# Attention with a selective bias, then a hard-swish MLP: the queries of the first eight pairs in another order

## The chip, the cores and the metric

The kernel runs on one core of a Trainium2 chip. The metric is the device time of one execution in microseconds, as the median of several executions. The engines are named as in the profile: PE multiplies matrices (PEld is its weight load), DVE is the vector engine, ACT the scalar engine, POOL is GpSimd, and SP issues DMAs. All of them run in the order of their own instruction lists and wait for each other by semaphores.

## The reference

Eight batches of eight heads attend causally over 576 tokens of 64 features. The scores carry a bias, minus the difference of running sums of the positive part of `s`, so a key far back in a stretch of large `s` counts less. The result, 4608 rows of 512, goes through two dense layers with a hard-swish between them.

```python
scores = scale * np.matmul(q, k.transpose(0, 1, 3, 2))        # scale = 1/8
cum = np.cumsum(np.maximum(s, 0.0), axis=-1)
bias = -(cum[:, :, :, None] - cum[:, :, None, :])
scores = np.where(causal, -1000000000.0, scores + np.minimum(bias, 0.0))
attn = softmax(scores)                                        # over the keys
x = (attn @ v) as rows of 512                                 # batch and token by head and feature
h = x @ w_in                                                  # 512 -> 2048
out = (h * np.clip(h + 3.0, 0.0, 6.0) / 6.0) @ w_out          # 2048 -> 512
```

## The kernel before

**Pairs.** The 64 heads are taken as 32 pairs `p`; four pairs make a batch of 576 rows. The loop `for p in range(NP)` (L773) writes out the order of work by hand; nothing reorders it. For each pair the queries and keys are loaded (`load_qk`, L109), turned so that features lie on partitions (`transpose_in` on PE, L229, then `transpose_out`, L249, out of PSUM into the tile `qk`), multiplied into scores (`scores`, L310, three groups a head of up to 512 columns, and `corner`, L369, for the last 64 tokens), exponentiated on ACT (L355), multiplied with the values (`av`, L401) and divided by their sums (`norm`, L429). The result `x` of a pair is turned back (`transpose_x`, L444) into `xT`. The loop fetches pair p+1 with `get(0)` (queries) and `get(1)` (keys) while pair p is scored, and does the second head's `av` and `norm` of pair p-1 there as well.

**Three kinds of pairs.** Pairs 0 to 10 (`NPE` is 11) are loaded six tokens to a row of a 96-row tile `tok`, in float16, by POOL's queue. Six PE transposes of 96x128 give a PSUM tile `pt` with two parities of tokens, one on partitions 0 to 63 and one on 64 to 127, and the copies out put them in order: each writes every second token in groups of three. Later pairs use a transposing DMA (`crossbar_qk`) and `spread` (L219). Pairs 0 to 7 (`NPROD` is 8) get their causal mask by product: PE first multiplies a constant tile `shut`, which holds -65504 where a key comes after its query, into the scores (L318, L374). Later pairs have `shut_out` on POOL put zeros in instead. Pairs from 8 on also use a tile of steps (`set_stair`).

**The bias.** Four rows of `qk` (partitions 64 to 67) hold the running sums of queries and keys, so the bias comes out of the same product as the scores. `rows_of` is where the sums are kept for all heads, with one slot for queries and one for keys; `load_aug` (L148) sends a head's rows from there by DMA. For pair 0 alone that would come too late, so its bias comes from a product with all rows (`by_rows`, L301), in which `picked` holds the sums of one head and zeros elsewhere: `pick_first` on ACT (L723) for head 0, `pick(1)` on DVE (L711) for head 1.

**The start.** The running sum over `s` is taken in two halves (`HALVES`, L54), the steps `cum1` to `cum6` (L671 to L702) alternating between ACT and DVE. POOL then copies the query sums into their slot (L747). Pair 0 is copied out head by head (`head_out`, L270), with ACT on three of the eight copies and DVE on five, DVE then does the pick (L756), and POOL goes on with `load_aug(1)`, the value cast of pair 0 (`cast_v`, L193), and further loads.

**Where the work overlaps.** In pairs 0 to 3 there is attention alone. From pair 4 on, `group()` puts one group of the MLP between the pieces of attention, either four matmuls into `ph` (L478, then ACT L493 and DVE L494 for the hard swish) or four into `po` (L505), in the order of the hand-written list `plan`. When a tile of 128 output rows is complete, DVE scales it into `ob` (L521) and SP's queue stores it (L524). SP's queue also issues the loads of values, the transposing DMAs and a few rows of sums; POOL's queue issues the loads that change type (queries and keys, weights) and most of the sums. `pool_mid` (L803) is POOL's share in the middle of a pair: the value cast, and for pairs 5 to 7 the tile of steps.

Of the kernel before, what the change touches and what calls it, by code (L numbers as in the profile page):

```python
# [18 lines left out]
def kernel(  # L19
# [32 lines left out]
    NROW = 1  # L52
    NWARM = (11, 2, 6)
    HALVES = (slice(0, 288), slice(288, SEQ))  # L54

# [35 lines left out]
    ident = keep("ident", [128, 128], F16)  # L91
    shut = keep("shut", [128, 640], F16)
    ident2 = keep("ident2", [128, 128], F16)
    stair_sb = keep("stair_sb", [128, 2, 128], F16)
    bias3 = keep("bias3", [128, 1], F32)
    rows_of = keep("rows_of", [128, 2, 640], F16, 2)
    sel = keep("sel", [128, 4], F32)
# [11 lines left out]
    def load_qk(p, i):  # L109
        b, h0 = p // PPB, 2 * (p % PPB)  # L110
        src = (q, k)[i][b, h0 : h0 + 2]
        if not flat(p):
            if not i:
                tok = work.tile([128, 24 * D], F16, tag="tok", bufs=4, name="tok")
                toks[p] = tok[0:96].rearrange("p (i h e d) -> p i h e d", i=2, h=2, e=6)
            nc.gpsimd.dma_start(
                out=toks[p][:, i].rearrange("p h e d -> p h (e d)"),
                in_=src.rearrange("h (p e) d -> p h (e d)", e=6),
            )
        else:  # L120
            if p < NSW:
                if not i:
                    tok = work.tile([128, 24 * D], F16, tag="tok", bufs=4, name="tok")
                    toks[p] = tok[:, 0 : 18 * D]
                to, eng = toks[p], nc.gpsimd
            else:
                to, eng = raws[p % NRAW], nc.sync
            eng.dma_start(
                out=to.rearrange("p (i t d) -> p i t d", i=2, t=9)[:, i],
                in_=src.rearrange("h s d -> (h s) d").rearrange(  # L130
                    "(t p) d -> p t d", p=128
                ),
            )
# [14 lines left out]
    def load_aug(p, eng):  # L148
        for hh in range(2):
            g = 2 * p + hh  # L150
            eng.dma_start(  # L151
                out=qks[p % NQK][64:68, hh, :, 64 * hh : 64 * hh + SEQ],
                in_=rows_of[g // 32].rearrange("(r g) i t -> g r i t", g=32)[
                    g % 32, :, :, 0:SEQ
                ],
            )
# [72 lines left out]
    def transpose_in(p, i):  # L229
        tok = toks[p]  # L230
        pt = t_bank(i == 1 and p != NPROD, "pt")
        if flat(p):
            for c in range(5):
                c0 = 512 * i + 128 * c
                nc.tensor.transpose(
                    pt[:, 128 * c : 128 * (c + 1)], tok[:, c0 : c0 + 128], ident
                )
            return pt
        for hh in range(2):
            for c in range(3):  # L240
# [6 lines left out]
        return pt  # L247

    def transpose_out(  # L249
        p, i, pt, copies=(nc.vector.tensor_copy, nc.vector.tensor_copy), pars=(0, 1)  # L250
    ):
        qk = qks[p % NQK]
        if flat(p):
            order(qk, i, pt.rearrange("p (t c) -> p t c", c=128), i, copies)
            return
        copies = (nc.scalar.copy if i else copies[0], copies[1])
        for par in pars:
            to = qk[0:64, 0, i, par : par + SEQ]
            copies[par](  # L259
# [9 lines left out]

    def head_out(p, i, hh, pt, copies):  # L270
        to = qks[p % NQK][0:64, hh, i, 64 * hh : 64 * hh + SEQ]
        for par in range(2):
            copies[par](
# [27 lines left out]
    def by_rows(p, hh, out, keys, queries, stop=False):  # L301
        mm(
            out,
            lhsT=rows_of[0][:, 1, keys],
            rhs=picked[:, 2 * p + hh, queries],
# [4 lines left out]
    def scores(p, hh, g):  # L310
# [4 lines left out]
        if g == 0:  # L315
            rows = slice(0, 68 if by_product else 128)
            if by_product:
                mm(S, lhsT=ident2, rhs=shut[:, 0:512], start=True, stop=False)  # L318
            for j in range(4):
# [12 lines left out]
        else:  # L332
# [10 lines left out]
            if p < NROW:  # L343
                for j in ((0, 3) if g == 1 else (1, 2)):
# [3 lines left out]
                        S[:, c : c + w],  # L348
                        lhsT=rows_of[0][:, 1, 128 * j : 128 * (j + 1)],
                        rhs=picked[:, 2 * p + hh, 128 * (j + 1) : SEQ],  # L350
# [18 lines left out]
    def corner(p):  # L369
# [3 lines left out]
        if by_product:  # L373
            mm(  # L374
                S.rearrange("p h c -> p (h c)"),
                lhsT=ident2,
                rhs=shut[:, 512:640],
                start=True,
                stop=False,
            )  # L380
# [117 lines left out]
    def m2(n, i):  # L498
# [13 lines left out]
        if fq == 3:  # L512
# [10 lines left out]
            )  # L523
            nc.sync.dma_start(out=out[r : r + 128, 0:w], in_=ob[:, 0:w])  # L524

# [82 lines left out]
    fill(nc.gpsimd, shut, 0.0)  # L608
    for c in (slice(0, 512), slice(512, 640)):
        w = 128 if c.start == 0 else 64  # L610
        part = shut[:, c].rearrange("p (t c) -> p t c", c=w)
        nc.gpsimd.affine_select(
            out=part,
            in_=part,
            pattern=[[0, (c.stop - c.start) // w], [1, w]],
            compare_op=ALU.is_ge,
            fill=-65504.0,
            base=0,
            channel_multiplier=-1,
        )  # L620

# [24 lines left out]
    fill(nc.gpsimd, rows_of[0][:, 0, :], 1.0)  # L646
    fill(nc.gpsimd, rows_of[0][:, 1, SEQ:640], 0.0)
    fill(nc.gpsimd, qks[0][64:68, 1, :, :], 0.0)
# [37 lines left out]
    def cum3(n, copy, cols):  # L686
        copy(out=rows_of[n][:, 1, cols], in_=C["c"][:, cols])

    def cum4(n, eng, cols):
        eng.tensor_tensor(  # L690
            out=C["r"][64:128, cols],
            in0=C["c"][64:128, cols],
            in1=rows_of[n][64:128, 1, cols],
            op=ALU.subtract,
        )

    def cum5(n, copy, cols):
        copy(out=rows_of[n][64:128, 1, cols], in_=C["r"][64:128, cols])

    def cum6(n, eng, cols):  # L700
        lo = rows_of[n][96:128, 1, cols]
        eng.tensor_tensor(out=lo, in0=C["r"][96:128, cols], in1=lo, op=ALU.subtract)  # L702
# [7 lines left out]

    def pick(g):  # L711
        nc.vector.tensor_scalar(
            out=picked[:, g, :],
# [10 lines left out]
    def pick_first(cols):  # L724
        nc.scalar.activation(
            out=picked[0:32, 0, cols],
            in_=C["c"][0:32, cols],
            func=AF.Identity,
# [7 lines left out]
    cum3(0, A, HALVES[1])  # L736
    fill(nc.gpsimd, rows_of[0][0:32, 1, 0:SEQ], -1.0)
    for i in range(2):
# [7 lines left out]
    pick_first(HALVES[1])  # L746
    nc.gpsimd.tensor_copy(out=rows_of[0][0:32, 0, 0:SEQ], in_=C["c"][0:32])  # L747
    pts = [transpose_in(0, 0)]
# [3 lines left out]
    head_out(0, 1, 0, pts[1], (V.tensor_copy, V.tensor_copy))  # L752
    head_out(0, 0, 1, pts[0], (A, V.tensor_copy))
    head_out(0, 1, 1, pts[1], (V.tensor_copy, V.tensor_copy))
    warm(NWARM[2])
    for g in range(1, 2 * NROW):  # L756
        pick(g)
    load_aug(1, nc.gpsimd)
# [14 lines left out]
    for p in range(NP):  # L773
# [58 lines left out]
        if PPB <= p < NPROD:  # L832
            pool_mid()
            if p == 4:
                load_aug(7, nc.gpsimd)
            elif p in (6, 7):
                load_aug(p + 2, nc.gpsimd)
# [5 lines left out]
        if p == 10:  # L843
            load_s(1, (nc.sync,) * 4)
            fill(nc.gpsimd, rows_of[1][:, 0, :], 1.0)

# [95 lines left out]
        elif p == 12:  # L942
            nc.scalar.copy(out=rows_of[1][0:32, 0, 0:SEQ], in_=C["c"][0:32])
            cum3(1, nc.scalar.copy, whole)
            fill(nc.gpsimd, rows_of[1][0:32, 1, 0:SEQ], -1.0)
        av(p, 0, 1)
# [43 lines left out]
```

The softmax here doesn't subtract the row's maximum and nothing guards it: scores larger than these inputs give would overflow.

## Time and profile before

| what | us |
|---|---|
| median of 3 runs (lowest, highest) | 356.13 (356.01, 356.2) |
| the profiled execution | 356.22 |
| its span, first to last instruction | 354.5 |
| PE busy in the span | 345.6 |
| DVE, ACT, POOL busy in the span | 231.5, 225.4, 169.6 |
| first score product of pair 0 (L318) | 8.95 |
| first score product of pairs 1, 2, 3, 4 (L318) | 14.26, 18.42, 22.68, 26.94 |

All times inside a profile count from the first instruction of the span. In lines of the timeline the columns are start, length, engine, line of the code, operation, what is written and read, shapes, count, and in brackets the idle time before with what ended it. In lines of waits they are who waited, for whom, total, times and longest. In group lines the busy time and the mean of one follow the bar, and then the idle time before them. An engine's name with a q is its sequencer or queue. The granted PE clock is 1.00 throughout. A busy PE isn't a PE at its peak, since matmuls overlap: a matmul of 512 columns shows 379 ns, but four in a row take 0.86 us.

### The profile page before, as it was taken

To read this page: it belongs to the slowest core of one execution; us is meant where nothing else is said; L and a number is where in the kernel's file an instruction comes from. 1 tells how busy PE (TensorE), PEld (TensorE's weight loads), DVE (VectorE), ACT (ScalarE), POOL (GpSimd) and SP (SyncE) were. 2 spreads that over 40 slices of the span, in tenths; PEclk is the share of its full clock that TensorE was granted. 3 is DMA by queue.
4 is the path that set the end of the run, shared out by engine and by line. 5 is a ranking of instruction groups with operands and counts; after the bars stand their busy time and mean duration, and the time that the engine had idled before them with its cause. 6 is when DMAs were issued, how large, how long until landed. Compare 5 with 4: busy or idle time off the path is not lost.

```text
span 354.5 us, 7771 instructions
## 1 busy us (share of the span) xinstructions
PE 345.6 (97%) x2926; PEld 191.5 (54%) x2926; DVE 231.5 (65%) x472; ACT 225.4 (64%) x397; POOL 169.6 (48%) x295
## 2 busy tenths in 40 slices
PE   7889999999999999999999999999999999999995
PEld 3676666655555555555555555555555444444442
DVE  7898897677878677666666665757654553544531
ACT  6897896787787666667766666666664344433310
POOL 8987799666779556555555555555310000000000
PEclk9999999999999999999999999999999999999999
DMA  9999999999999999998788969997120100101111
GB/s 164 156 219 209 186 184 175 104 187 183 146 126 140 190 219 187 160 214 178 174 176 189 179 162 187 175 176 164 39 75 12 59 31 31 59 2 59 59 58 63
DMA packets 144438, 48.35 MB, mean 136 GB/s; under 512 B 130696, under 2 KB 139432, under 8 KB 144400
## 3 DMA queue, kind: packets, MB, share of 16 engines
q1 hardware_dynamic: 117088, 37.52, 53.4%
q0 software_dynamic: 27072, 10.05, 25.4%
q8 instruction: 23, 0.38, 0.5%
q10 hardware_dynamic: 240, 0.28, 0.2%
q14 instruction: 15, 0.12, 0.1%
HBM read 37.36 MB, written 9.44 MB: 132 GB/s over the span
## 4 chain that ended last, share of the span: by engine, by line
PE 90%; DVE 4%; ACT 3%; issue 1%; DMA 1%; ACTq 0%
PE po L505 34%; PE ph L478 34%; PE O L412 8%; PE S L336 7%; PE S L321 4%; DVE qk L259 1%; PE pt L242 1%; ACT P L355 1%; PE ptx L449 1%; DMA s_all<-in_s_dram 1%; DVE x L435 1%; PE S L318 1%; ACT tr L493 1%; DVE qk L219 1%; PE Sc L385 0%
## 5 line engine op out<-in xcount | busy, mean ns | idle before, releaser
L494 DVE SCALAR_TENSOR_TENSOR gT<-tr,ph 128x512 f16<-128x512 f32 x144 | 98.9, 687 | 97.4 <-ACT tr L493 96.3
L478 PE MATMUL ph<-xT,w_in_sb 128*128 128x512 f16 x576 | 148.1, 379 | 0.0
L505 PE MATMUL po<-w_out_sb,gT 128*128 128x512 f16 x576 | 145.8, 379 | 0.0
L493 ACT ACTIVATE tr<-ph,bias 128x512 f32<-128x512 f32 x144 | 99.1, 688 | 73.0 <-PE ph L478 70.6
L355 ACT ACTIVATE P<-S 128x512 f16<-128x512 f32 x192 | 111.4, 596 | 37.4 <-PE S L321 22.2
L478 PEld LDWEIGHTS <-w_in_sb 128*128 128x128 f16 x576 | 51.6, 97 | 44.2
L505 PEld LDWEIGHTS <-gT 128*128 128x128 f16 x576 | 50.2, 97 | 46.4 <-issue 0.2
L359 POOL TENSOR_SCALAR_AFFINE_SELECT P<-P 128x512 f16<-128x512 f16 x48 | 31.2, 650 | 45.2 <-ACT P L355 45.1
L336 PE MATMUL S<-qk 68*128 68x448 f16 (+3 forms) x256 | 49.0, 272 | 0.3 <-ACT P L355 0.2
L412 PE MATMUL O<-va,P 128*128 128x65 f16 x896 | 47.9, 193 | 0.3 <-ACT P L355 0.3
L412 PEld LDWEIGHTS <-P 128*128 128x128 f16 x896 | 39.3, 97 | 14.0 <-ACT P L355 0.5
L219 DVE COPY qk<-jt 64x768 f16<-64x768 f16 x84 | 36.6, 437 | 1.2
L336 PEld LDWEIGHTS <-qk 68*128 68x128 f16 x256 | 23.7, 98 | 24.2 <-issue 0.7
L151 POOL DMA_DIRECT2D qk<-rows_of x58 | 34.1, 591 | 2.8 <-PE S L336 1.6
L435 DVE TENSOR_TENSOR x<-O,rl 128x320 f16<-128x320 f32 x64 | 31.5, 492 | 2.2
L521 DVE TENSOR_SCALAR ob<-po 128x512 f32<-128x512 f32 (+1 forms) x36 | 24.4, 676 | 8.3 <-PE po L505 7.6
L259 DVE COPY qk<-pt 64x576 f16<-64x576 f16 x30 | 24.0, 805 | 6.4 <-ACT qk L259 5.3
L359 POOL TENSOR_SCALAR_AFFINE_SELECT PC<-PC 128x128 f16<-128x128 f16 x24 | 7.1, 294 | 41.0 <-ACT PC L393 40.9
L321 PEld LDWEIGHTS <-qk 128*128 128x128 f16 (+1 forms) x256 | 18.9, 98 | 12.7 <-DVE qk L259 0.8
L321 PE MATMUL S<-qk 128*128 128x128 f16 (+1 forms) x256 | 24.8, 219 | 0.0
L195 POOL CAST va<-vraw 128x512 f16<-128x512 f32 x32 | 21.2, 664 | 3.4 <-DMA vraw<-in_v_dram 3.3
L191 POOL CAST tok<-raw 128x576 f16<-128x576 f32 x28 | 18.1, 681 | 0.0
(71 smaller groups left out, 197.4 us busy)
## 6 DMA issues: line engine op xcount, KB each, us to landing
out_dram<-ob SPq DMA_DIRECT2D x35, 256.0 KB, 2.2
vraw<-in_v_dram SPq DMA_DIRECT2D x64, 128.0 KB, 3.8
raw<-in_q_dram SPq DMA_DIRECT2D x14, 288.0 KB, 3.7
raw<-in_k_dram SPq DMA_DIRECT2D x14, 288.0 KB
tok<-in_q_dram POOLq DMA_DIRECT2D x18, 144.0 KB, 4.9
tok<-in_k_dram POOLq DMA_DIRECT2D x18, 144.0 KB, 6.0
w_in_sb<-in_moe_w_in_dram POOLq DMA_DIRECT2D x4, 512.0 KB, 8.7
w_out_sb<-in_moe_w_out_dram POOLq DMA_DIRECT2D x8, 256.0 KB, 7.4
```

Source lines behind the costliest of these rows:

```text
L151: eng.dma_start(out=qks[p % NQK][64:68, hh, :, 64 * hh : 64 * hh + SEQ], in_=rows_of[g // 32].rearrange("(r g) i t -> g r i t", g=32)[g % ...
L219: copies[par](out=qk[0:64, :, i, 128 * par : 128 * par + 256 * n].rearrange("p h (s two c) -> p h s two c", two=2, c=128)[:, :, :, 0, :], ...
L321: mm(S[:, c], lhsT=kT[rows, c], rhs=qT[rows, c], start=(j == 0 and not by_product), stop=(j == 3 and p >= NROW),)
L336: mm(S[:, c : c + w], lhsT=kT[0:68, 128 * j : 128 * (j + 1)], rhs=qT[0:68, 128 * (j + 1) : SEQ], start=(c == 0), stop=(c != 0 and p >= NROW),)
L355: nc.scalar.activation(out=pt[:, c], in_=S, func=AF.Exp, scale=0.125)
L359: nc.gpsimd.affine_select(out=part, in_=part, pattern=[[0, part.shape[1]], [1, w]], compare_op=ALU.is_ge, fill=0.0, base=0, channel_multip ...
L412: mm(o[:, i, :], lhsT=lhsT, rhs=va[:, hh, j, 0:65], **kw)
L435: nc.vector.tensor_tensor(out=X[p][:, :, hh, :], in0=o[:, :, 0:64], in1=rl.to_broadcast([128, 5, 64]), op=ALU.mult,)
L478: mm(ph, lhsT=w_in_sb[:, kc, ft * 128 : (ft + 1) * 128], rhs=xT[:, kc, n * 512 : (n + 1) * 512], start=(kc == 0), stop=(kc == NKC - 1),)
L493: nc.scalar.activation(out=tr, in_=ph, func=AF.Relu, bias=bias3[:, 0:1])
L494: nc.vector.scalar_tensor_tensor(out=gTs[n][:, ft, :], in0=tr, scalar=6.0, in1=ph, op0=ALU.min, op1=ALU.mult)
L505: mm(po, lhsT=gTs[n][:, ft, t4 * 128 : (t4 + 1) * 128], rhs=w_out_sb[:, ft, :], start=(ft == 0), stop=(ft == NFT - 1),)
```

## The change

For pairs 0 to 7 the queries stand in another order inside each group of 64: position 16w + v of a group holds token 4v + w. Four neighbouring tokens are loaded to a row in place of six, in three blocks of 96 rows. The PE transposes write runs of 16 columns into `pt`, and the copies out then read without steps and write runs of 16 neighbours. Keys stay in token order. What depends on the query's place follows it: the mask `shut` (now one 128x128 tile, read four times over through a step of 0), the picks, and the query sums in `rows_of`, which gets a third slot, so that slot 0 holds the reordered query sums for pairs 0 to 7, slot 1 the plain ones for later pairs (filled on POOL in pair 5) and slot 2 the key sums. The rows of `x`, and so of the output, of the first two batches come out in the new order; their stores, two for each tile of 128 rows, put every row back in its place.

Three things move beside it. The pick for pair 0's second head goes from DVE to POOL, right behind the copy of the query sums and ahead of `load_aug(1)`. ACT's first copy for head 1 of pair 0 goes to DVE. In the key copies of pairs 1 to 10, ACT copies the first parity of one head and DVE that of the other, where ACT did both; the second parity stays on DVE. The first half of the running sum has 320 columns instead of 288.

```diff
-    HALVES = (slice(0, 288), slice(288, SEQ))
+    HALVES = (slice(0, 320), slice(320, SEQ))
...
-    shut = keep("shut", [128, 640], F16)
+    shut = keep("shut", [128, 128], F16)
...
-    rows_of = keep("rows_of", [128, 2, 640], F16, 2)
+    rows_of = keep("rows_of", [128, 3, 640], F16, 2)
...
+            if mixed(p, i):
+                nc.gpsimd.dma_start(
+                    out=toks[p][:, i]
+                    .rearrange("p h e d -> p (h e d)")
+                    .rearrange("p (t x) -> p t x", t=3),
+                    in_=src.rearrange("h s d -> (h s) d").rearrange(
+                        "(t p e) d -> p t (e d)", p=96, e=4
+                    ),
+                )
+                return
...
+        if mixed(p, i):
+            for t in range(3):
+                for c in range(2):
+                    nc.tensor.transpose(
+                        pt[:, 0:SEQ].rearrange("p (g c v) -> p c g v", c=2, v=16)[
+                            :, c, 6 * t : 6 * t + 6
+                        ],
...
+    def mixed(p, i):
+        return i == 0 and p < NPROD
+
+    def mix(ap):
+        return ap.rearrange("p (g w v) -> p g w v", w=4, v=16)
+
+    def unmix(ap):
+        return ap.rearrange("p (g v w) -> p g w v", w=4, v=16)
...
-        copies = (nc.scalar.copy if i else copies[0], copies[1])
+        if i:
+            head_out(p, i, 1, pt, (nc.scalar.copy,), (0,))
+            head_out(p, i, 0, pt, (nc.vector.tensor_copy,), (0,))
+            pars = (1,)
         for par in pars:
+            if mixed(p, i):
+                to = qk[0:64, 0, i, 16 * par : 16 * par + SEQ]
+                copies[par](
+                    out=bass.AP(
+                        to.tensor,
+                        to.offset,
+                        [list(to.ap[0]), [2 * SPAD + 64, 2], [32, 18], [1, 16]],
+                    ),
+                    in_=pt[64 * par : 64 * par + 64, 0:SEQ].rearrange(
+                        "p (h g v) -> p h g v", h=2, v=16
+                    ),
+                )
+                continue
...
-                mm(S, lhsT=ident2, rhs=shut[:, 0:512], start=True, stop=False)
+                mm(
+                    S.rearrange("p (t c) -> p t c", c=128),
+                    lhsT=ident2,
+                    rhs=shut[:, None, :].to_broadcast([128, 4, 128]),
+                    start=True,
+                    stop=False,
+                )
...
-            nc.sync.dma_start(out=out[r : r + 128, 0:w], in_=ob[:, 0:w])
+            if r < NPROD // PPB * SEQ:
+                for g in range(2):
+                    nc.sync.dma_start(
+                        out=out[r + 64 * g : r + 64 * g + 64, :].rearrange(
+                            "(v w) d -> w v d", w=4
+                        ),
+                        in_=ob[64 * g : 64 * g + 64, :],
+                    )
+            else:
+                nc.sync.dma_start(out=out[r : r + 128, 0:w], in_=ob[:, 0:w])
...
-    def pick(g):
-        nc.vector.tensor_scalar(
+    def pick(g, eng):
+        eng.tensor_scalar(
             out=picked[:, g, :],
...
         nc.scalar.activation(
-            out=picked[0:32, 0, cols],
-            in_=C["c"][0:32, cols],
+            out=mix(picked[0:32, 0, cols]),
+            in_=unmix(C["c"][0:32, cols]),
...
-    nc.gpsimd.tensor_copy(out=rows_of[0][0:32, 0, 0:SEQ], in_=C["c"][0:32])
+    nc.gpsimd.tensor_copy(
+        out=mix(rows_of[0][0:32, 0, 0:SEQ]), in_=unmix(C["c"][0:32])
+    )
+    for g in range(1, 2 * NROW):
+        pick(g, nc.gpsimd)
...
-    head_out(0, 0, 1, pts[0], (A, V.tensor_copy))
+    head_out(0, 0, 1, pts[0], (V.tensor_copy, V.tensor_copy))
     head_out(0, 1, 1, pts[1], (V.tensor_copy, V.tensor_copy))
     warm(NWARM[2])
-    for g in range(1, 2 * NROW):
-        pick(g)
...
+            elif p == 5:
+                fill(nc.gpsimd, rows_of[0][:, 1, :], 1.0)
+                nc.gpsimd.tensor_copy(
+                    out=rows_of[0][0:32, 1, 0:SEQ], in_=C["c"][0:32]
+                )
```

## The prediction

> **What bounds the kernel now.** I read the first part of the page, then PE's idle time by cause, then DVE and POOL in order of time, each for the stretch that the one before pointed to.
>
> The page, its totals and its last chain by engine:
>
> ```profile
> span 354.5 us, 7771 instructions
> ...
> PE 345.6 (97%) x2926; PEld 191.5 (54%) x2926; DVE 231.5 (65%) x472; ACT 225.4 (64%) x397; POOL 169.6 (48%) x295
> ...
> PE 90%; DVE 4%; ACT 3%; issue 1%; DMA 1%; ACTq 0%
> ```
>
> PE has the end of the kernel in its hands, and the change leaves PE's work as it is (as many matmuls of as many columns). It can only pay where PE waits. In 34 to 110 us only five steps between consecutive matmuls exceed the time of their columns (four of 512 columns take 0.86 us in the chain, 0.42 ns a column) by 0.1 us or more, the largest by 0.37. So all there is lies before 34 us. PE's waits there:
>
> ```profile
> PE ptx L449 <- DVE x L435: 1.3, 3, 0.5
> PE Sc L302 <- DVE w_out_sb L712: 0.7, 1, 0.7
> ...
> PE S L336 <- ACT P L355: 0.2, 1, 0.2
> ```
>
> Start to start, with columns taken off, the stalls are 0.82 us at 11.93 (pair 0's corner, for the second pick); 0.55, 0.61 and 0.62 before the transposes of x at 17.82, 22.08 and 26.34; 0.17 at 28.93; 0.49 at 31.77; 0.29 at 33.63: 3.55 us, the ceiling for any gain here. DVE in that stretch, in order of time:
>
> ```profile
> 9.77 1.51 DVE L273 COPY qk<-pt 64x288 f16<-64x288 f16 x3 [0.46 <-ACT qk L273]
> 11.31 0.57 DVE L712 TENSOR_SCALAR w_out_sb<-rows_of,sel 128x576 f16<-128x576 f16 x1
> 11.91 2.31 DVE L259 COPY qk<-pt 64x576 f16<-64x576 f16 x3
> 14.46 0.20 DVE L434 RECIPROCAL rl<-O 128x5 f32<-128x5 f32 x1 [0.24 <-PE O L412]
> 14.69 0.49 DVE L435 TENSOR_TENSOR x<-O,rl 128x320 f16<-128x320 f32 x1
> 15.38 1.63 DVE L259 COPY qk<-pt 64x576 f16<-64x576 f16 x2 [0.19 <-PE pt L242]
> 17.04 0.20 DVE L434 RECIPROCAL rl<-O 128x5 f32<-128x5 f32 x1
> 17.27 0.49 DVE L435 TENSOR_TENSOR x<-O,rl 128x320 f16<-128x320 f32 x1
> 17.80 0.81 DVE L259 COPY qk<-pt 64x576 f16<-64x576 f16 x1
> 18.63 0.46 DVE L454 COPY xT<-ptx 128x576 f16<-128x576 f16 x1
> ```
>
> From 15.38 to 28.88 DVE has no idle piece over 0.04 us: a pair takes 4.26 us (its S starts at 14.26, 18.42, 22.68, 26.94), while PE needs about 3.4 us of columns. DVE sets the pace for pairs 1 to 4. Two prices stand side by side in the groups:
>
> ```profile
> L259 DVE COPY qk<-pt 64x576 f16<-64x576 f16 x30 | 24.0, 805 | 6.4 <-ACT qk L259 5.3 <-PE pt L242 0.6
> L454 DVE COPY xT<-ptx 128x576 f16<-128x576 f16 x9 | 4.1, 454 | 0.6 <-PE ptx L449 0.5
> ```
>
> Same source memory, type and 576 elements: 805 ns where each written element is two places from the last, 454 ns where they are neighbours.
>
> **The change, part by part.** Durations are of the profiled execution (356.22 us, span 354.5, so 1.72 lie outside the span); it stands 0.09 us over the median of 356.13.
>
> Query copies, pairs 0 to 7. In the new order both sides run over neighbours in runs of 16. By the two rows a 64x576 copy costs 0.454 to 0.805; I take 0.46, since the contiguous row shares memory, type and neighbour step, and only the runs differ. That is 0.35 less, twice a pair: -0.70 on DVE. A 64x288 copy is now 0.48 (0.30 of elements and 0.18 fixed) and becomes 0.33.
>
> Key copies, pairs 1 to 10. ACT copies one head instead of two: 0.80 becomes 0.47 (its 64x288 row), -0.33. DVE takes the other half: +0.48 and 0.03 between, +0.51 a pair. Net on DVE: -0.19 for pairs 1 to 7; for 8 to 10, whose queries are unchanged, +0.51, and that is covered by DVE's idle share (28.4 busy of 40 us in 60 to 100); uncovered it would cost 1.5 in all.
>
> Start-up. The first half of the prefix sum has 320 columns, not 288. A scan of 288 takes 0.758 and of 576 takes 1.348: +0.07 for 32, and about +0.03 on each of ACT's first-half steps, against shorter second halves; I put +0.10 on the first scores (bounds 0 and 0.2). The strided first pick on ACT costs 0.53 today for either half; the row nearest for another pattern of its size is the 0.43 cast, so -0.1 to +0.1, taken as none. Then DVE: today 2.60 us from 9.31 to 11.91 (a 0.46 wait for ACT's copy, three copies, the pick). After: two copies of 0.33, two of 0.48, 0.12 between, 1.74, with no wait, because both parities of head 1's queries are DVE's own. DVE is free 0.76 earlier (0.86 less 0.10), and pair 0's second corner can run at about 11.20 in place of 11.93: -0.73.
>
> The pick on POOL. Queue today:
>
> ```profile
> 8.45 0.68 POOL L747 CAST rows_of<-c 32x576 f16<-32x576 f32 x1
> 9.43 1.18 POOL L151 DMA_DIRECT2D qk<-rows_of  x2 [0.29 <-POOL rows_of L747]
> 10.61 0.63 POOL L195 CAST va<-vraw 128x512 f16<-128x512 f32 x1
> ```
>
> POOL's smaller mask (memset 0.41 to 0.15, selects 0.63 and 0.29 to one of 0.29) saves 0.9 us earlier, but the memset of -1 waits for ACT at 6.92 in any case, so the L747 copy still starts near 8.55. POOL has no multiply by a column in this trace; its rows nearest in size are 0.63 to 0.65 (128x512 select and cast) and 1.25 (copy of 64x1280). I take 0.72, the 512-element rows scaled to 576, range 0.6 to 1.25. The reordered L747 reads every fourth element: 0.68 as now to 1.25, taken as 0.68. So the pick ends near 10.0, before the 11.20 where PE wants it. What it is moved past: both row loads of pair 1 are issued about 0.6 later (the 0.29 wait goes), at 10.0 and 10.6, and by today's 2.8 us to landing arrive at 12.8 and 13.4; PE wants the first at 13.74 (14.47 less 0.73). The v cast of pair 0 ends at 12.05, and PE wants it at 12.6. The query/key loads of pairs 3 and 4 land at 15 to 19.6, four microseconds before use. So 0.55 us of slack (v), 0.94 (rows): beyond it every microsecond on POOL is one on PE.
>
> [...]
>
> Pairs 1 to 4, by DVE's lead over today. PE runs without a wait from 11.93 to 15.35, so DVE's waits for O at 14.46 and for pt at 15.38 come 0.73 earlier. Pair 2's queries: -1.43, and x is there before PE asks: the 0.55 stall goes. Pair 2's keys give 0.51 back: -0.92, and now PE waits for these at the first score product of pair 2, which is what is late next. Pair 3: -1.62, then -1.11. Pair 4: -1.81, then -1.30. So PE gains 1.30 by pair 4's scores; the 0.17 at 28.93 stays (same engine, same order). ACT then sets the pace from 31.13 to 33.58, with the key copy in it:
>
> ```profile
> 32.34 0.80 ACT L259 COPY qk<-pt 64x576 f16<-64x576 f16 x1
> 32.98 0.60 ACT L355 ACTIVATE P<-S 128x512 f16<-128x512 f32 x1
> ```
>
> 0.33 less there removes the 0.29 stall at 33.63. The 0.49 at 31.77 stays. Sum: 0.73 + 3 x 0.70 - 3 x 0.51 + 0.29 = 1.59.
>
> Costed at nothing, with their cover: query loads of 288 rows in place of 192 (1152 rows take 1.06 us of POOL, 192 take 0.67, so +0.04 each; pair 0's key tile lands at 7.34, and DVE is not free for it before 8.33). The extra fill and copy of pair 5 on POOL: 0.36 + 0.68 = 1.04 at 40.7, in front of two query/key loads, the w_out loads, the v cast and row loads of pair 8. Those rows land at 54.02 and are used at 58.26, so with both shifts 1.6 are left; the last w_out piece lands at 61.90, its product starts at 64.54, the piece itself 0.43 later: with both shifts 0.4 is left, the thinnest cover. Stores: nine tiles go out in two issues, +0.35 to 0.54 of SP each; the transposing load behind the first lands at 74.02 for a use at 76.16. A store lands in 2.2 us today; one three times as long still frees its buffer, needed again three tiles later, in time (the first four go out at 66.70, 72.27, 87.09 and 90.85). [...] Transposes written in runs of 16, and the mask read with step 0, keep their columns; no row shows either, bounds 0 to 0.05 us a transpose set, hidden but for DVE's pace.
>
> **The rivals.**
> R1, the neighbour copies don't run at the fast rate (runs of 16 break it). For it: no row has such short runs. Against: the 454 ns row. Place: DVE, 15 to 27 us. The start-up lead is 0.43 (0.73 less 0.30 for the two copies of 288), pair 1's keys then end at 14.43, when today's reciprocal starts, so that only the 0.19 idle before 15.38 is left of it; pairs 2 to 4 cost 3 x 0.51 = 1.53, ACT gives 0.29: slower by 1.05, 357.2. At a price c of one copy, a pair changes by 2(c - 0.805) + 0.51; three pairs eat the 1.02 of start-up and ACT at c = 0.72, and from there it decides.
> R2, POOL is late: both its operations at 1.25 are 1.10 more than taken, 0.55 of it slack: 0.55 lost, 355.1. With the pick at 2 us, 355.9; for slower than before they must exceed 3.5 together.
> R3, given back later: the w_out piece or the SP queue arrives late now that PE is early. Up to 1.0 of POOL's 1.04 less 0.4: 355.2.
> R4, the keys don't hold pairs 2 to 4 back, because DVE's copies overlap more than today's: then all three stalls before x go, 0.73 + 1.78 + 0.29 = 2.80, 353.3. Against: DVE keeps about 4.07 us a pair (4.26 - 0.19), over PE's 3.4.
>
> **How the numbers follow.** 356.22 - 1.59 = 354.63, less 0.09 to the median: 354.6 as forecast, own range 354.0 to 355.2. Chances: forecast 0.55, R1 0.12, R2 0.15, R3 0.10, R4 0.08. The range drops R1 (0.12) and the far ends of R2 and R4: 353.5 to 356.6. A change within 0.2% (0.71 us) can't be told from none: 355.4 to 356.8 is same. Faster: forecast and R4 0.63, and some 0.09 of R2 and R3: 0.72. Slower: R1 and a little of R2: 0.13. Same: 0.15.
>
> **What would show it.** Right: L259's mixed form on DVE near 0.46; no wait for L712 at the corner; the waits of ptx for x replaced by waits of the first score products for the key copies; S of pair 4 at about 25.6 instead of 26.94; pairs at 4.07 us. Wrong: 0.8 us copies (R1); PE waiting for va or for pair 1's rows at 12 to 15 us (R2); PE gaps at 40 to 70 us on w_out or row loads (R3).

## The result and the profile after

The changed kernel takes 369.55 us (median; 368.52 to 371.91) against 356.11 (356.01 to 356.2): slower by a factor of 1.0387, interval 1.0333 to 1.044. The forecast was 354.6. The profiled execution took 368.52 us, with a span of 366.8 against 354.5, 12.3 us more. The page, its totals and its last chain by engine and by line:

```profile
span 366.8 us, 7795 instructions
...
PE 347.5 (95%) x2926; PEld 192.0 (52%) x2926; DVE 227.5 (62%) x482; ACT 222.8 (61%) x396; POOL 172.6 (47%) x297
...
PE 67%; DMA 14%; DVE 6%; SPq 6%; issue 2%; ACT 2%; POOL 2%; ACTq 0%; POOLq 0%
PE po L567 27%; PE ph L540 26%; DMA jt<-tok 10%; PE O L474 5%; PE S L398 5%; PE S L383 2%; SPq L342 2%; DMA s_all<-in_s_dram 2%; DMA vraw<-in_v_dram 2%; SPq L138 2%; DVE gT L556 1%; DVE qk L229 1%; DVE x L497 1%; SPq L588 1%; ACT P L417 1%
```

PE is busy no longer than before to within 2 us, but the chain that ended last is PE for 67% where it was 90%, and `jt<-tok`, the transposing loads of queries and keys of the later pairs, holds 10% of it, where DMA as a whole had 1%. To see when, I compared the starts of the same matmul in both traces (negative: after is earlier):

```
start of the same matmul, before -> after, us
pair 0, second corner             11.93 -> 11.83    -0.10
second head of pair 1             16.23 -> 16.50    +0.27
second head of pair 2             20.43 -> 20.41    -0.02
second head of pair 3             24.68 -> 24.39    -0.29
second head of pair 4             31.81 -> 31.21    -0.60
first scores of pair 5            35.02 -> 34.13    -0.89
first scores of pair 7            49.39 -> 48.30    -1.09
later, near 83 / 92 / 103 / 165 us       -1.0 / +3.3 / +5.4 / +12.7
```

So the change had won 1.09 us by the scores of pair 7, the last of the reordered pairs, and then lost some 13.7 between 83 and 165 us, where the attention it changed is over and only the nine tiles with the new stores remain. PE's and DVE's waits after (who, for whom, total, times, longest):

```profile
PE ph L540 <- DVE gT L556: 9.1, 4, 5.0
PE S L398 <- ACT P L417: 2.2, 2, 2.0
```

```profile
DVE qk L229 <- DMA jt<-tok: 23.1, 11, 7.5
...
DVE x L497 <- DMA xT<-x: 3.4, 3, 2.0
```

The first layer (`ph`) waits for DVE's hard swish (`gT`), and DVE is not slow: it stands in front of `spread` (L229) with nothing else in its list until a transposing load has landed, 23.1 us in eleven waits that the trace of before does not have. (The transposing DMAs of `x`, on the same queue, cost it another 3.4.) One of these waits, in the chain of work that ended last (start, length, what):

```profile
95.69 1.08 SPq L588
...
96.81 0.03 SPq L342
96.84 0.03 issue
96.87 10.55 DMA jt<-tok
...
107.45 0.35 DVE qk L229
...
108.13 0.70 DVE gT L556
...
108.87 1.02 PE ph L540 x4
```

L588 is the reordered store. SP issues its second half in 1.08 us and the transposing load behind it at once, but the load lands 10.55 us after the start of its issue. In before, the loads of this line (L286 there) whose landing the trace tells took:

```profile
DMA to landing us min/median/max: 3.2/5.2/6.8
```

The largest stall, 5.17 us of PE at 156.59, has the same two lines ahead of it: a store at 144.87 and a transposing load at 148.43.

The early part, in DVE's order of time, against the stretch that the prediction showed:

```profile
10.11 0.99 DVE L329 COPY qk<-pt 64x288 f16<-64x288 f16 x2
11.14 0.92 DVE L295 COPY qk<-pt 64x576 f16<-64x576 f16 x2
12.86 0.48 DVE L329 COPY qk<-pt 64x288 f16<-64x288 f16 x1 [0.81 <-ACT qk L329]
13.36 0.81 DVE L307 COPY qk<-pt 64x576 f16<-64x576 f16 x1
14.74 0.20 DVE L496 RECIPROCAL rl<-O 128x5 f32<-128x5 f32 x1 [0.57 <-PE O L474]
14.96 0.49 DVE L497 TENSOR_TENSOR x<-O,rl 128x320 f16<-128x320 f32 x1
```

and in the groups, shapes kept apart:

```profile
L295 DVE COPY qk<-pt 64x576 f16<-64x576 f16 x14 | 6.3, 452 | 0.8 <-PE pt L252 0.6
L307 DVE COPY qk<-pt 64x576 f16<-64x576 f16 x16 | 12.9, 806 | 0.2
L780 POOL TENSOR_SCALAR w_out_sb<-rows_of,sel 128x576 f16<-128x576 f16 x1 | 1.7, 1728 | 0.1
L815 POOL CAST rows_of<-c 32x576 f16<-32x576 f32 x1 | 1.2, 1236 | 0.0
```

The reordered query copies (L295) run at 452 ns beside 806 of the second-parity key copies (L307): the core of the change does what it says. The two POOL operations are both well above what was taken (1.73 for 0.72, 1.24 for 0.68).

### The profile page after: what moved, and what is told of

Read it like the earlier page. It is cut to its first block, busy times and chain, and to the rows that moved or that the text cites. A ratio compares the mean times of both kernels' runs of the same rounds, so it can differ in the third digit from the quotient of the medians.

```text
span 366.8 us, 7795 instructions
## 1 busy us (share of the span) xinstructions
PE 347.5 (95%) x2926; PEld 192.0 (52%) x2926; DVE 227.5 (62%) x482; ACT 222.8 (61%) x396; POOL 172.6 (47%) x297
## 4 chain that ended last, share of the span: by engine, by line
PE 67%; DMA 14%; DVE 6%; SPq 6%; issue 2%; ACT 2%; POOL 2%; ACTq 0%; POOLq 0%
PE po L567 27%; PE ph L540 26%; DMA jt<-tok 10%; PE O L474 5%; PE S L398 5%; PE S L383 2%; SPq L342 2%; DMA s_all<-in_s_dram 2%; DMA vraw<-in_v_dram 2%; SPq L138 2%; DVE gT L556 1%; DVE qk L229 1%; DVE x L497 1%; SPq L588 1%; ACT P L417 1%
## 5 line engine op out<-in xcount | busy, mean ns | idle before, releaser
L556 DVE SCALAR_TENSOR_TENSOR gT<-tr,ph 128x512 f16<-128x512 f32 x144 | 98.5, 686 | 86.7 <-ACT tr L555 85.5
L229 DVE COPY qk<-jt 64x768 f16<-64x768 f16 x84 | 33.9, 405 | 24.3 <-DMA jt<-tok 23.1
L205 POOL CAST va<-vraw 128x512 f16<-128x512 f32 x32 | 21.2, 661 | 24.2 <-DMA vraw<-in_v_dram 24.1
L421 POOL TENSOR_SCALAR_AFFINE_SELECT PC<-PC 128x128 f16<-128x128 f16 x24 | 7.2, 299 | 23.1 <-ACT PC L455 22.9
L307 DVE COPY qk<-pt 64x576 f16<-64x576 f16 x16 | 12.9, 806 | 0.2
```

Source lines behind the costliest of these rows:

```text
L229: copies[par](out=qk[0:64, :, i, 128 * par : 128 * par + 256 * n].rearrange("p h (s two c) -> p h s two c", two=2, c=128)[:, :, :, 0, :], ...
L421: nc.gpsimd.affine_select(out=part, in_=part, pattern=[[0, part.shape[1]], [1, w]], compare_op=ALU.is_ge, fill=0.0, base=0, channel_multip ...
L556: nc.vector.scalar_tensor_tensor(out=gTs[n][:, ft, :], in0=tr, scalar=6.0, in1=ph, op0=ALU.min, op1=ALU.mult)
```

## The experiments

**The stores alone, and everything but the stores.** Two kernels cut the change in two. The first is after with the store of before:

```diff
-            if r < NPROD // PPB * SEQ:
-                for g in range(2):
-                    nc.sync.dma_start(
-                        out=out[r + 64 * g : r + 64 * g + 64, :].rearrange(
-                            "(v w) d -> w v d", w=4
-                        ),
-                        in_=ob[64 * g : 64 * g + 64, :],
-                    )
-            else:
-                nc.sync.dma_start(out=out[r : r + 128, 0:w], in_=ob[:, 0:w])
+            nc.sync.dma_start(out=out[r : r + 128, 0:w], in_=ob[:, 0:w])
```

> The changed kernel with the store of before for all tiles: one issue of 128 rows, in the order in which they come, so the rows of the first two batches are not put back in their places. If the loss lies in the stores (theories A, B and C), the lead of 0.9 us that the changed kernel's PE still has at 71 us stays to the end: 355.2, and no wait of DVE for jt. If it lies elsewhere, in POOL's extra work of pair 5 or in DVE's larger share of the key copies (theory D): still about 369.

The second is before with the stores of after, and nothing else:

> The kernel before with the changed kernel's stores alone, two issues of 64 rows for each of the first nine tiles, with 4 as the slowest dimension; its queries are in token order, so these rows land in wrong places. Theories A to C (the stores): slower by the 13 to 15 us that the changed kernel lost, 368 to 371, with DVE waiting for jt. Theory D: 356 to 356.5.

Measured: 356.14 us for the first (ratio 1.001, 0.9987 to 1.0033), 370.72 for the second (1.0395, 1.0344 to 1.0445). The stores carry the whole loss. The first has the lead of 1.09 us at 48 to 60 us and 0.70 of it from 83 us to the end, and in it DVE never waits for `jt`. In the second, with the attention of before, DVE waits again:

```profile
DVE qk L219 <- DMA jt<-tok: 19.4, 7, 7.3
```

**What in the stores.** They differ from the plain ones in three things: two issues a tile, rows scattered over the output, and a slowest dimension of 4. Three kernels put one issue a tile into before and change only the size `w` of the slowest dimension (rows land scattered in all three):

```diff
-            nc.sync.dma_start(out=out[r : r + 128, 0:w], in_=ob[:, 0:w])
+            if r < NPROD // PPB * SEQ:
+                nc.sync.dma_start(
+                    out=out[r : r + 128, :].rearrange("(v w) d -> w v d", w=16),   # then 4, then 8
+                    in_=ob,
+                )
+            else:
+                nc.sync.dma_start(out=out[r : r + 128, 0:w], in_=ob[:, 0:w])
```

> The kernel before with one issue a tile, its rows scattered with 16 as the slowest dimension (rows land in wrong places). Theory A, the number of DMA engines that share a store, taken from its slowest dimension: 16 engines as before, 355.9 to 356.5. Theory B, the doubled issues: one issue, so 356 as well. Theory C, that rows written out of order are slow in themselves: 362 or more.

> The kernel before with one issue a tile, its rows scattered with 4 as the slowest dimension (rows land in wrong places). Theory A: 4 engines carry 256 KB, packets in flight at once at most 8 where there were 15 to 20, the transposing loads behind wait as in the changed kernel, 365 to 371. Theory B: one issue, about 356. Theory C: the same time as with 16 as the slowest dimension.

> The kernel before with one issue a tile, rows scattered with 8 as the slowest dimension (rows land in wrong places). Theory A: twice the engines of 4, packets in flight at once about 10 to 12, each pair of stores done in half the 10 us, and a loss well under half of 17 us, because the later loads' slack of about 2 us covers most: 356.5 to 360. If the number of engines weren't taken from that dimension: as with 4 (373) or as with 16 (356.2).

Measured: 356.17 us for 16 (ratio 1.0, 0.9991 to 1.001), 360.25 for 8 (1.0115, 1.009 to 1.014), 373.02 for 4 (1.0448, 1.0393 to 1.0504). One issue with 4 is no faster than two, and the same scatter with 16 costs nothing: neither the issues nor the scatter is the cause, the size of the slowest dimension is. Of the transposing loads, who waited for them, and their time from issue to landing (minimum, median, maximum), with 16, 8 and 4:

```profile
DMA to landing us min/median/max: 3.5/4.9/6.8
```

```profile
  DVE qk L219: 11.3, 9
...
DMA to landing us min/median/max: 4.6/5.8/9.5
```

```profile
  DVE qk L219: 26.2, 10
...
DMA to landing us min/median/max: 4.3/5.8/10.9
```

With 16 nobody waits; with 8 DVE waits 11.3 us, with 4 26.2. The trace tells the landing of two of the nine stores: 4.0 and 4.1 us with 16, where the same two took 3.1 and 3.3 in before; that costs nothing. What hurts is what a store does to the loads behind it. Counted from the trace's packets over the first eight tiles, a tile's 128 rows are in flight at most 15 to 20 at a time in before and 17 to 22 with 16, 9 to 11 with 8, and 5 to 8 in after and 5 to 7 with 4; from its first packet to its last a tile takes 0.9 to 2.0 us in before and 3.9 to 5.8 in after. So fewer rows are in flight at a time, the smaller the slowest dimension. In the chain above, the store issued at 95.01 moves its packets from 98.5 to 103.6, and the load issued behind it lands at 107.42. Theory A puts both down to the number of DMA engines that share a store; that is not shown, since the packets in the trace do not name their engine.

**Another place for the rows.** If the stores have to be plain, the order must be undone elsewhere. The first layer's moving operand can be read in token order (for the first eight tiles; the ninth keeps its two stores):

```diff
+            cols = xT[:, kc, n * 512 : (n + 1) * 512]
+            if n < 2:
+                cols = cols.rearrange("p (g w v) -> p g v w", w=4, v=16)
             mm(
-                ph,
+                ph if n >= 2 else unmix_out(ph),
...
-                rhs=xT[:, kc, n * 512 : (n + 1) * 512],
+                rhs=cols,
```

Three more kernels were built on it: one with the pick back on DVE, one with pair 5's extra POOL work ahead of the value cast as well, and one in which ACT copies the first parity of both heads' keys again.

> [...] If the stores are the whole loss and a moving operand read in steps of 32 bytes costs nothing: like the run with plain stores, 355.3 to 356.2 with executions up to 361, four ph matmuls in a row in 0.86 us. If such a read runs at half rate: 128 matmuls by 0.215 us more, 27 us slower.

> The same with the second pick back on DVE, behind the head copies. Theory E (POOL is late from the start: 1.24 us for the reordered sums and 1.73 for the pick, so the queue of POOL stays 1.4 us behind until 64 us, and the few slow executions come from there): the wait for va at 13.6 us goes, the wait of O for PC at 63.9 us goes, 354.9, and no execution above 356. Theory F (the spread has another cause): the spread stays, and the median moves by less than 0.3.

> The same, with POOL's fill and copy of pair 5 ahead of its value cast, where POOL waited 3.3 us for a load in the kernel before. Theory E: 0 to 0.3 us less than with the pick on DVE alone, 354.7, and the w_out pieces and row loads land 1 us earlier. Theory F: no difference.

> The same, with ACT copying the first parity of both heads' keys as in the kernel before, so that the key copies cost DVE 0.51 us less and ACT 0.33 more a pair. Theory G (DVE sets the pace of pairs 1 to 4, and the split gives back on the keys what the queries won): the waits of the first score products for the key copies go, pair 4's scores start 0.5 to 1.0 earlier, 354.0 to 354.3. Theory H (the split pays for itself on ACT): no earlier, or later by up to 0.3 at 33.6 us, 354.7 to 355.0.

Measured: 464.09 us (ratio 1.3015), 467.81, 466.76 and 467.92. The cost is in the first layer, from PE's timeline and the view by stretches (length, busy time of PE, PEld, DVE, ACT and POOL with counts, granted PE clock, DMA share, GB/s):

```profile
27.42 2.81 PE L546 MATMUL ph<-xT,w_in_sb 128*128 128x512 f16 x3
30.05 0.40 PE L401 MATMUL S<-qk 68*128 68x448 f16 x2
```

```profile
25.00:30.00 5.00, 4.80 (x50) 2.11 (x48) 3.29 (x8) 2.44 (x5) 2.91 (x7) 1.00 1.29 217
```

```profile
60.00:80.00 20.00, 20.00 (x84) 7.37 (x83) 6.02 (x13) 6.59 (x12) 8.66 (x12) 0.50 0.55 84
```

At a granted clock of 1.00 three matmuls of 512 columns take 30.05 - 27.42 = 2.63 us, 0.88 each, where they take 0.215 when their columns are neighbours (four in 0.86). From 35 to 100 us the clock is granted at 0.50, and they still take 0.88 (four from 62.80 to 66.34); products with neighbouring columns double: the two score products of 448 and 64 columns take 0.42 at 71.73 and, in the changed kernel at 12.82 and a granted clock of 1.00, 0.22. So the strided read sets the 0.88, not the clock, and the lower clock comes on top for everything else. Nothing about the pick, pair 5 or the keys can be told from times in which this is the term that counts.

**The order undone in the turn of x.** `transpose_x` multiplies by a unit matrix; a permuted one turns and reorders at the same price (218 ns a product against 220, in the run with the pick on DVE below). Pair 7's `x`, which before goes by a transposing DMA, has then to be turned by PE too:

```diff
+    perm = keep("perm", [128, 128], F16)
...
-                ident,
+                perm if p < NPROD else ident,
...
+    nc.gpsimd.tensor_copy(out=unmix(perm), in_=mix(ident))
...
-        if PPB < p < NPROD:
+        if PPB < p <= NPROD:
             transpose_x(p - 1)
```

Stores plain; pair 5's extra work was put ahead of its value cast. On top of it, one kernel has the pick on DVE, and one has ACT's key copies whole besides.

> The changed kernel with plain stores and its rows put back where x is turned, by a permuted unit matrix in place of the unit matrix (pair 7 by PE too), and with POOL's work of pair 5 ahead of its value cast; the second pick stays on POOL. If the order costs nothing there: the plain-store run less the 0.47 us that PE waited for POOL at 63.9, so 354.9 to 355.6 by the median. Theory E (slow executions come from POOL being 1.4 us behind since the start) leaves some spread here, since the pick's 1.73 us remain.

> The same with the second pick on DVE, behind the head copies. Theory E: PE's lead at 27 us grows from 0.9 to about 1.46, as the runs with the order in the matmuls already had it at that point, and it stays: 354.6, spread under 0.5. Theory F (another cause): spread as in the run with plain stores, up to 361.

> The same, and ACT copies the first parity of both heads' keys again. Theory G (the split gives back on DVE what the queries won): lead at 27 us 1.6 to 2.0, 354.1 to 354.5. Theory H (the split pays on ACT at 33 us): 354.6 or more.

Measured: 361.36 us (1.0127 to 1.0165), 359.3 and 359.1. These were slowed by my two additions. PE's waits in the first:

```profile
PE ptx L512 <- DVE qk L308: 1.9, 1, 1.9
PE S L384 <- DMA qk<-rows_of: 1.5, 1, 1.5
...
PE po L568 <- DMA w_out_sb<-in_moe_w_out_dram: 0.8, 2, 0.6
```

Pair 7's `ptx` stands in a PSUM bank that a copy of keys has yet to empty (1.9 us). POOL's fill, moved forward, waits for a load of rows, 2.1 us in the first run and 4.1 in the second, and the loads behind it come late: in the first run by 4.1 us against the run with plain stores (46.70 for 42.61), of which some 3 were there before the fill. The keys made no difference that can be told beside this.

**The same without the two additions.** Pair 7's `ptx` goes to a bank of scores, and pair 5's work back to where the change has it. Then one step at a time: the pick on DVE in place of POOL; pair 5's extra work done at the start; ACT's key copies whole.

```diff
-    for g in range(1, 2 * NROW):
-        pick(g, nc.gpsimd)
...
     head_out(0, 1, 1, pts[1], (V.tensor_copy, V.tensor_copy))
     warm(NWARM[2])
+    for g in range(1, 2 * NROW):
+        pick(g, nc.vector)
```

```diff
-    fill(nc.gpsimd, rows_of[0][:, 0, :], 1.0)
+    fill(nc.gpsimd, rows_of[0][:, 0:2, :], 1.0)
...
+    A(out=rows_of[0][0:32, 1, 0:SEQ], in_=C["c"][0:32])
...
-            elif p == 5:
-                fill(nc.gpsimd, rows_of[0][:, 1, :], 1.0)
-                nc.gpsimd.tensor_copy(
-                    out=rows_of[0][0:32, 1, 0:SEQ], in_=C["c"][0:32]
-                )
```

```diff
-        if i:
-            head_out(p, i, 1, pt, (nc.scalar.copy,), (0,))
-            head_out(p, i, 0, pt, (nc.vector.tensor_copy,), (0,))
-            pars = (1,)
+        copies = (nc.scalar.copy if i else copies[0], copies[1])
```

> The changed kernel, rows put back by a permuted unit matrix where x is turned, plain stores; pair 7 turned by PE into a bank of the scores. Pick and pair 5's work on POOL as in the changed kernel. Theory E (POOL's lateness): level with the run with plain stores, 355.4 to 356.5, single executions up to 361, waits of PE at 55 to 65 us for row loads, w_out or a select of POOL. Theory F (the spread came with something else in that run): 355.1, spread under 0.5.

> The same with the second pick on DVE behind the head copies. Theory E: POOL is 1.7 us earlier from 12 us on, PE leads by 1.6 at 50 us, 354.6 to 355.0, with less spread. Theory F: as with the pick on POOL, less 0.5 from the start-up alone.

> The same, and the plain query sums for later pairs are written at the start, the ones by POOL's fill there, the sums by ACT between its two head copies and its first exponential, so that pair 5's 1.04 us on POOL are gone. Theory E: another 0 to 0.4 less, 354.4 to 354.8, spread under 0.5. Theory F: no difference, or 0.1 more for ACT at the start.

> The same, and ACT copies the first parity of both heads' keys, as in the kernel before. Theory G (the split gives back on DVE what the queries won): PE leads by 1.8 or more at 25 us, 354.0 to 354.4. Theory H (the split pays, because ACT is the later one where it matters): 354.6 to 355.4.

Measured: 356.42 us with the pick on POOL (1.0001 to 1.0033); 355.58 with it on DVE (0.9979 to 0.9996); 355.60 with pair 5's work at the start (0.9981 to 0.9998); 356.18 with whole key copies (0.9999 to 1.0017); the intervals are those of the ratio to before. So by the medians the pick on POOL costs 0.84 us, pair 5's work on POOL nothing, and the split of the key copies earns some 0.6. The whole copies keep the lead at 24.9 us (0.97 against 0.93), and lose it where ACT has the work: ACT has no gap between 12.7 and 26 us, and a stall of 0.49 appears at 32.75. PE's waits at 55 to 70 us, with the pick on POOL and on DVE (the first profile is of an execution of 357.86 us, 1.4 above its median, so the sizes are those of a late one):

```profile
PE O L475 <- POOL PC L422: 0.7, 1, 0.7
PE po L571 <- DMA w_out_sb<-in_moe_w_out_dram: 0.5, 1, 0.5
PE O L475 <- POOL P L422: 0.4, 1, 0.4
```

```profile
PE ptx L515 <- ACT P L418: 0.2, 1, 0.2
PE O L475 <- POOL PC L422: 0.2, 1, 0.2
```

**The pick on DVE, with plain stores and no reordering back** gives the same answer without the turn of x:

> The changed kernel with plain stores (the rows of the first two batches are not put back) and the second pick on DVE, pair 7 by the transposing DMA. If the transposes of pair 7 by PE took the lead of the run with the pick on DVE: lead 1.6 at 56 us and at least 1.2 after 65, 354.8 to 355.1. If the late stage takes it in any case: a lead of 0.4 to 0.7 after 65, 355.4 to 355.6.

Measured: 354.77 us (0.9959 to 0.9989), some 1.3 less than the 356.1 with the pick on POOL.

**A version that keeps what pays.** The turn of pair 7 by PE is not free. In the run with pair 5's work at the start, PE is 1.72 us ahead of before at 60 us and 0.47 at 66; between them stands `ptx` of pair 7, in a bank of scores that ACT is still reading:

```profile
PE ptx L515 <- ACT P L418: 0.5, 1, 0.5
```

So seven pairs are reordered and put back by the permuted unit matrix; pair 7 stays in token order, with its own small mask and by its transposing DMA; stores are plain, the pick is on DVE, pair 5's work is at the start. Against the run with pair 5's work at the start, in part:

```diff
+    NMIX = NPROD - 1
...
     def mixed(p, i):
-        return i == 0 and p < NPROD
+        return i == 0 and p < NMIX
...
-                    rhs=shut[:, None, :].to_broadcast([128, 4, 128]),
+                    rhs=shuts[p >= NMIX][:, None, :].to_broadcast([128, 4, 128]),
...
-                perm if p < NPROD else ident,
+                perm if p < NMIX else ident,
```

> Seven reordered pairs instead of eight, rows put back where x is turned by PE, pair 7 in token order with a mask of its own and the transposing DMA, plain stores, pick on DVE, plain query sums written at the start. If pair 7's transposes were the cost: 354.7 to 355.1, the best of all. If not: 355.4 to 355.6, or 0.2 more for pair 7's query copies at 0.81 instead of 0.46.

Measured: 354.85 us (354.73 to 358.44), ratio 0.9981 (0.9964 to 0.9999): 14.7 us less than the changed kernel, and 1.28 less than before by the medians, with an interval that ends just below 1. It is 0.75 less than with pair 7 turned by PE (355.60), and level with the 354.77 of the run that does not put the rows back, so undoing the order costs nothing that can be told. Its page, and all of PE's waits of 0.3 us or more:

```profile
span 353.0 us, 7785 instructions
...
PE 344.7 (98%) x2926; PEld 191.3 (54%) x2926; DVE 231.4 (66%) x483; ACT 223.1 (63%) x397; POOL 170.3 (48%) x297
...
PE 89%; DVE 5%; ACT 3%; issue 1%; DMA 1%; ACTq 0%
```

```profile
PE W L710 <- DVE one L716: 1.3, 1, 1.3
PE pt L268 <- DMA tok<-in_k_dram: 0.7, 1, 0.7
PE S L386 <- DVE qk L310: 0.4, 2, 0.2
PE S L386 <- ACT qk L325: 0.3, 1, 0.3
PE Sc L361 <- DVE w_out_sb L786: 0.3, 1, 0.3
PE O L477 <- ACT P L420: 0.3, 1, 0.3
```

The three waits of `ptx` for `x` are gone, and its lead, 1.47 us at 47 to 56 us, is still 1.45 at the end. In all these variants, this one too, some executions take 1 to 5 us longer; the two profiles of such executions (357.86 with the pick on POOL and pair 7 turned by PE, 357.77 with plain stores and the pick on DVE) show waits for POOL and for weights at 55 to 70 us. Why only some executions have them was not found.

## Why the prediction was wrong, and where it was right

**The step that failed: the stores, costed at nothing.** The text gave them "two issues, +0.35 to 0.54 of SP each" and asked only whether a store three times as long "still frees its buffer"; the size of the slowest dimension has no term in its sum, and 4, 8 and 16 measured +16.9, +4.2 and 0.0 us. The buffer did come free; the work that mattered was behind the store on SP's queue, the transposing loads, one of which the same sentence names with its slack: landing at 74.02 for a use at 76.16. That slack of 2.1 us was held against a later issue, 0.35 to 0.54, and never against a slower landing. The load in the chain above then landed 10.55 us after issue, where 6.8 had been the longest, DVE stood 23.1 us before such loads, and `gT` and so `ph` stood behind DVE. The cover to be named was the slack of every load on that queue.

**R3, "given back later",** named SP's queue as a place and was the rival that came true in kind, but with a price of 0.6 us (355.2 against 354.6), taken from POOL's work; the price here is 13.7. The POOL work of pair 5 that this price came from costs nothing (355.58 against 355.60).

**The copies: right.** 0.46 was taken for the reordered query copy, 0.452 measured; R1 falls. The 64x288 form took 0.30 where 0.33 was taken; the split of its 0.48 into 0.30 and 0.18 was my estimate (the rows of 576 and 288 elements, 0.805 and 0.480, differ by 0.325). The transposes that write runs of 16 took 206 ns each where those of before took 206, and the mask product that reads with step 0 took 379 where 378 was.

**The pick on POOL: mis-sized.** 0.72 was taken, the row of a select and cast, and 1.73 measured, above the upper bound of 1.25; the reordered copy took 1.24, close to its upper bound of 1.25. Together 1.57 over what was taken. DVE was done with pair 0's copies at 11.10, as forecast, but the pick ended at 11.78, so that the second corner came at 11.83 and not 11.20, and the value cast behind it (L205) ended at 13.58, so that PE's first product with the values came at 13.63, 0.37 after its turn. So R2 came true beside the stores, and its arithmetic was near: 0.63 and 0.37 are 1.0 us lost at the start, where 1.57 less its 0.55 of slack gives 1.02. POOL in order of time:

```profile
8.71 1.24 POOL L815 CAST rows_of<-c 32x576 f16<-32x576 f32 x1
10.05 1.73 POOL L780 TENSOR_SCALAR w_out_sb<-rows_of,sel 128x576 f16<-128x576 f16 x1
11.75 1.21 POOL L161 DMA_DIRECT2D qk<-rows_of  x2
12.96 0.62 POOL L205 CAST va<-vraw 128x512 f16<-128x512 f32 x1
```

Nor did DVE win by being rid of it: DVE's line above has a wait of 0.81 for ACT's key copy of pair 1 just behind, so that the pick's 0.50 falls into it (with the pick on DVE, in the last version, that copy starts at 12.78 against 12.86, without a wait). The prediction counted the pick's 0.57 as won on DVE's way to pair 1; there it was not on the path. At pair 0's corner it is: with the pick on DVE, PE still waits 0.34 for it (11.76 in the last version).

**Pairs 1 to 4: right in kind, mis-sized.** The second heads gain 0.27 to 0.31 a pair over before (0.27, -0.02, -0.29, -0.60 in the table) where 0.19 was forecast; the 0.1 between them is not explained. The waits of `ptx` went and the first score products wait for the keys in their place (0.37 at 22.62, 0.36 at 26.59), as forecast; R4 falls. Pair 4's S starts at 26.01, forecast about 25.6; in the last version, with the pick on DVE, it starts at 25.57. The split key copies cost DVE what was said and bring 0.6 in all.

**The sum beside the stores.** By the scores of pair 7 the lead was 1.09, where the sum said 1.59. By the second heads, 0.27 was lost at the start where 0.73 was to be won, 0.87 won over pairs 1 to 4 where 0.57 was forecast, and 0.49 behind them where 0.29 was. The last version reaches 1.47, close to 1.59, by 0.17, 0.88 and 0.42: errors that offset each other, so this closeness is luck. (The prediction's own subtraction gives 354.54, which it wrote as 354.6; nothing hangs on that.)

## What to carry to other kernels

When the pattern of a DMA changes, ask what is queued behind it and how much slack that has, not only who waits for the DMA itself; where fewer of its rows go at a time (here 5 to 8 in flight for 15 to 20), price the next transfer, not this one. Here the order was undone for nothing that can be told where a multiplication by a unit matrix already stood (354.85 us against 354.77), and the turn that had to be added for pair 7 cost 0.75. An operation moved to another engine saves only what lay on the path there, and is to be priced by a row of its own kind (the pick on POOL: 0.72 taken, 1.73 measured, 0.84 us of the kernel).

## What the hardware showed that I had not expected

- Nine stores of 128 rows of 2 KB cost the kernel 0.0, 4.2 and 16.9 us together with a slowest dimension of 16, 8 and 4, and what came late was the transposing loads behind them on the same queue, which landed after up to 6.8, 9.5 and 10.9 us.
- A matmul whose moving columns lie 32 bytes apart takes 0.88 us for 512 columns, 4.1 times the 0.215 of neighbouring ones, at a granted clock of 1.00 and of 0.50 alike. The first of them starts at 27.42 at a clock of 1.00; from 35 to 100 us the granted clock is 0.50, although the profile shows PE busy throughout.
- POOL's multiplication by a column took 1.73 us for 128x576 in float16, DVE's 0.50 (the last version) and 0.57 (before); POOL's copy of 32x576 out of float32 took 1.24 with reads 16 bytes apart and 0.68 with neighbours.
